# Attention and MoE in one kernel: 512-byte runs for the first loads, w_out behind granules 3 and 4, one exp for two heads, a longer MoE lag

## The chip, the cores and the metric

The kernel runs on one core of a Trainium2 chip. Times are microseconds (us) of device time. Repeated executions of one kernel on one chip mostly agreed within about 1%. A "span" is the length of the one profiled execution; the measured time of that execution is about 1.8 us longer. In the profile, PE is TensorE's matmuls, PEld its weight loads, DVE is VectorE, ACT ScalarE, POOL GpSimd, and SP the engine that issues most transfers of the hardware queue.

## The reference

```python
# attention: B=4, H=8, S=768, D=64; causal window of 96 keys plus 8 global keys, ALiBi bias
scores = q @ k.T / sqrt(D) - slope[h] * dist          # masked outside window and globals
x = softmax(scores) @ v                               # -> (3072 tokens, 512)
# "MoE" with one expert: 512 -> 2048 -> 512
r = relu(x @ w_in)
out = (s * r * r + b) @ w_out
```

Inputs are fp32; the kernel works in bf16 with fp32 sums. The term `b @ w_out` is the same for every token: b times the column sums of w_out, called `bvec` below.

## The kernel before

Tokens are cut into 12 granules of 256; a batch has three. A granule has four "units" (pairs of heads), and a step s treats two units, so a granule takes two steps. q and k of a granule must be transposed before the scores: by TensorE for the first granules, later by DMA. The attention output xn must be transposed to xT for the first MoE product (p1, eight pieces of 8 matmuls per granule). The second product (p2, two halves of 16 matmuls) follows.

```python
    # loads: q/k of granules 0 and 1 as fp32 on two hardware queues, 256-byte runs
    for j in range(2):
        for i in range(GB):
            for n, eng in enumerate((nc.sync, nc.scalar)):
                f = work.tile([P, H, D], F32, name="first", ...)
                eng.dma_start(f[:], rows_of(srcs[n], 0, j * GB + i))
    nc.scalar.preload_act_table_set("natural_log_exp_and_others")
    # ... (constants)
    # everything else by GpSimd's queue, which also casts to bf16, in this order:
    #   v of granules 0, 1;  w_in (4 pieces);  w_out (4 pieces);  granules 2, 3;  later 4, 5, ...

    def post(hi):                      # per head, after the scores of a unit
        nc.scalar.activation(pt[:, 0:ncol], pss[hi][:, 0:ncol], ACT.Exp, scale=QSCALE)
        nc.vector.tensor_tensor(pv, pv, m, ALU.mult)        # mask and bias template

    def step(s, c0, c1, c2):           # c0, c1, c2: MoE pieces put between attention pieces
        j = 2 * s // HP
        last = (2 * s + 2) % HP == 0
        if not last and QK_PE <= j + 2 < NJ:
            qk_by_dma(j + 2)
        run(scores(s + 1))
        ...
        stage_A(2 * s)                 # probabilities @ v, division -> xn
        run(c1)
        stage_A(2 * s + 1)
        run(c2[0:1])
        if last:
            finish_granule(j)          # xT[j]: by TensorE if j < 3, else by DMA; loads granule j+4
        run(c2[1:])

    # ... granules 0, 1 (attention), p1[0], p1[1] with the sums of w_out's rows, p2[0], bvec,
    #     p2[1] mixed with granule 2's attention, granule 3 ...
    for j in range(4, NJ):             # steady part: p1 of the granule just finished
        step(2 * j,     p2[j - 2][0:1], p1[j - 1][0:2], p1[j - 1][2:4])
        step(2 * j + 1, p2[j - 2][1:2], p1[j - 1][4:6], p1[j - 1][6:8])
    run(p2[NJ - 2]); run(p1[NJ - 1]); run(p2[NJ - 1])
```

Each engine executes its instructions in the order in which they are written here.

The softmax here doesn't subtract the row's maximum and nothing guards it: scores larger than these inputs give would overflow.

## Time and profile before

| | before |
|---|---|
| median | 249.51 us (3 runs, 249.46 to 250.19) |
| span | 246.8 us |
| TensorE busy | 218.8 us, 89% |
| VectorE, ScalarE busy | 62%, 43% |

The head of the profile page: span, busy time of the engines, then the busy share of TensorE and its granted clock in tenths, in 40 slices of 6.2 us.

```profile
span 246.8 us, 4975 instructions
...
PE 218.8 (89%) x1955; PEld 145.8 (59%) x1978; DVE 154.1 (62%) x397; ACT 105.6 (43%) x201; POOL 64.5 (26%) x81
...
PE   8768979977987759939989999999999999999993
...
PEclk9995999995899989997999999999999999999999
```

The right half of the TensorE row is nines: there TensorE is the bound, and the timeline repeats one step every 8.0 us. The left half has holes. The waits of TensorE (what it waited for: us in total, times, longest) name the largest:

```profile
PE ps_1297 L387 <- DMA xT<-xn: 4.1, 1, 4.1
PE ps_1557 L387 <- DMA xT<-xn: 4.0, 1, 4.0
PE ps_s L299 <- DVE koff L262: 2.4, 2, 1.9
...
PE ps_1806 L387 <- DMA xT<-xn: 1.1, 1, 1.1
```

A wait has an afterpiece. In TensorE's timeline (start, us, what, count; in brackets the idle time ahead), the 8 matmuls of one p1 piece take 0.87 us from start to start when all is well:

```profile
84.90 0.19 PE L341 MATMUL ps_av<-voff,pt 128*128 128x65 bf16 x1
89.20 1.03 PE L387 MATMUL ps_1297<-xT,w_in_bf 128*128 128x256 bf16 x8 [4.10 <-DMA xT<-xn]
90.07 1.69 PE L387 MATMUL ps_1308<-xT,w_in_bf 128*128 128x256 bf16 x8
91.55 0.26 PE L341 MATMUL ps_av<-vb_88,pt 128*128 128x65 bf16 x1
```

The second piece needs 1.48 us (90.07 to 91.55) because the granted clock fell after the wait.

GpSimd's timeline tells when loads land. It held at most eight loads in flight: before it issues the next, it waits for the one issued eight earlier (the ninth load, at 10.67 us, waits for the first). Here its loads of granule 2 wait for the first and second piece of w_in:

```profile
19.23 0.89 POOL L92 DMA_DIRECT2D nat<-in_k_dram  x1 [1.78 <-DMA w_in_bf<-in_moe_w_in_dram]
22.40 0.88 POOL L92 DMA_DIRECT2D nat<-in_q_dram  x1 [2.28 <-DMA w_in_bf<-in_moe_w_in_dram]
```

**A count of lost time.** To compare kernels by stage I count, in each stretch of 10 us, TensorE's weight loads by kind, multiply each by the time it takes where TensorE is dense (p1 0.109 us, p2 0.2155, scores 0.0345, probabilities times v 0.031, transposes 0.055, all read from dense stretches of the timeline), and call the rest of the 10 us lost. Weight loads are counted because some matmul records are missing from this trace (1955 matmuls against 1978 loads). Before, 45.0 us are lost in the first 140 us: 32.2 ahead of 80 us, 12.8 behind.

### The profile page before, as it was taken

The numbers are of one execution on the slowest core, as the hardware profiler recorded it, in microseconds if no ns is written. First come the engines' busy times: TensorE is split into PE (matmuls) and PEld (weight loads), VectorE is DVE, ScalarE is ACT, GpSimd is POOL, SyncE is SP. The second block draws the span as 40 slices with busy tenths as digits, with TensorE's granted clock in tenths as the row PEclk, the third lists the DMA queues.
The fourth block names the chain that finished last, engine by engine and source line by source line (L and its number), as shares of the span: only waits on it lengthen the run. The fifth ranks groups of instructions, "written<-read, shape, count | busy, mean of one in ns | idle before, by whom it ended". The sixth has DMA issues, their size and how long they took to land.

```text
span 246.8 us, 4975 instructions
## 1 busy us (share of the span) xinstructions
PE 218.8 (89%) x1955; PEld 145.8 (59%) x1978; DVE 154.1 (62%) x397; ACT 105.6 (43%) x201; POOL 64.5 (26%) x81
## 2 busy tenths in 40 slices
PE   8768979977987759939989999999999999999993
PEld 3334968443565445717647756776677666774851
DVE  3478869974799616632566767665577686542431
ACT  0924746006076415603446446634474457330520
POOL 8632428986097500923320000000000000000000
PEclk9995999995899989997999999999999999999999
DMA  8999999999999994999995143252341303113102
GB/s 152 190 186 207 206 197 155 152 177 189 143 138 158 154 160 51 97 153 136 127 107 108 43 78 97 66 108 84 68 106 46 85 3 85 45 43 87 44 0 86
DMA packets 110071, 27.85 MB, mean 113 GB/s; under 512 B 102880, under 2 KB 106976, under 8 KB 110048
## 3 DMA queue, kind: packets, MB, share of 16 engines
q0 software_dynamic: 70784, 12.59, 70.0%
q1 hardware_dynamic: 35104, 13.90, 28.2%
q10 hardware_dynamic: 4160, 1.05, 2.3%
q8 instruction: 15, 0.25, 0.5%
q14 instruction: 8, 0.07, 0.1%
HBM read 27.26 MB, written 6.29 MB: 136 GB/s over the span
## 4 chain that ended last, share of the span: by engine, by line
PE 71%; DMA 13%; DVE 8%; ACT 3%; issue 2%; POOL 1%; SPq 1%; POOLq 0%; ACTq 0%; DVEq 0%
DMA xT<-xn 9%; PE ps_s L299 4%; DMA vb_87<-in_v_dram 4%; PE ps_av L341 4%; ACT pt L310 2%; PE ps_2775 L423 1%; PE ps_1641 L423 1%; PE ps_2290 L423 1%; PE ps_2156 L423 1%; PE ps_1389 L423 1%; PE ps_3027 L423 1%; PE ps_2904 L423 1%; PE ps_2656 L423 1%; PE ps_2531 L423 1%; PE ps_2408 L423 1%
## 5 line engine op out<-in xcount | busy, mean ns | idle before, releaser
L387 PEld LDWEIGHTS <-w_in_bf 128*128 128x128 bf16 x768 | 73.6, 100 | 21.0 <-issue 8.8
L396 DVE TENSOR_TENSOR gT<-gT 128x512 bf16<-128x512 bf16 x96 | 40.4, 424 | 41.8 <-ACT gT L395 39.5
L423 PEld LDWEIGHTS <-gT 128*128 128x128 bf16 x384 | 36.5, 99 | 43.1 <-issue 2.1
L310 ACT ACTIVATE pt<-ps_s 128x512 bf16<-128x512 f32 (+1 forms) x96 | 45.7, 576 | 29.9 <-PE ps_s L299 29.9
L92 POOL DMA_DIRECT2D nat<-in_k_dram x20 | 18.0, 900 | 23.0 <-DMA qk<-nat 15.3
L341 PEld LDWEIGHTS <-pt 128*128 128x128 bf16 x352 | 17.5, 101 | 9.9 <-DVE xn L350 1.9
L92 POOL DMA_DIRECT2D nat<-in_q_dram x20 | 18.0, 898 | 6.1 <-DMA w_in_bf<-in_moe_w_in_dram 3.9
L350 DVE TENSOR_TENSOR xn<-ps_av,rc 128x256 bf16<-128x256 f32 x43 | 18.2, 424 | 1.5
L299 PE MATMUL ps_s<-qk 64*128 64x128 bf16 x224 | 14.9, 228 | 2.8 <-ACT pt L310 2.3
L98 POOL DMA_DIRECT2D vb_88<-in_v_dram x12 | 10.6, 895 | 19.0 <-PE ps_av L341 18.7
L299 PEld LDWEIGHTS <-qk 64*128 64x128 bf16 x224 | 8.2, 97 | 9.5 <-issue 8.3
L98 POOL DMA_DIRECT2D vb_87<-in_v_dram x12 | 11.2, 938 | 6.3 <-DMA w_out_bf<-in_moe_w_out_dram 3.4
L341 PE MATMUL ps_av<-voff,pt 128*128 128x65 bf16 x116 | 11.6, 198 | 0.0
L299 PE MATMUL ps_s<-qk,koff 64*128 64x128 bf16 x128 | 9.4, 237 | 2.4 <-DVE koff L262 2.4
L140 PE MATMUL ps_w<-idle 128*128 128x512 bf16 x30 | 10.0, 478 | 1.5 <-DVE idle L134 1.2
L349 DVE RECIPROCAL rc<-ps_av 128x4 f32<-128x4 f32 x43 | 7.5, 174 | 4.9 <-PE ps_av L341 4.9
L341 PE MATMUL ps_av<-vb_88,pt 128*128 128x65 bf16 x112 | 9.0, 195 | 1.6 <-DVE xn L350 1.6
L404 DVE TENSOR_TENSOR wsum<-wsum,w_out_bf 128x512 f32<-128x512 f32 x14 | 9.6, 685 | 0.2
L341 PE MATMUL ps_av<-vb_87,pt 128*128 128x65 bf16 x88 | 7.8, 198 | 1.2 <-DMA vb_87<-in_v_dram 0.6
L299 PEld LDWEIGHTS <-koff 64*128 64x128 bf16 x128 | 5.5, 104 | 2.8 <-DVE koff L262 2.8
L140 PEld LDWEIGHTS <-idle 128*128 128x128 bf16 x32 | 3.4, 116 | 6.0 <-issue 3.2
L316 DVE TENSOR_TENSOR pt<-pt,tmpl_160 128x512 bf16<-128x512 bf16 (+1 forms) x12 | 4.8, 402 | 3.4 <-ACT pt L310 3.0
(314 smaller groups left out, 363.2 us busy)
## 6 DMA issues: line engine op xcount, KB each, us to landing
out_dram<-o_sb SPq DMA_DIRECT2D x24, 256.0 KB, 2.3
nat<-in_k_dram POOLq DMA_DIRECT2D x20, 128.0 KB, 7.7
nat<-in_q_dram POOLq DMA_DIRECT2D x20, 128.0 KB, 7.5
w_in_bf<-in_moe_w_in_dram POOLq DMA_DIRECT2D x4, 512.0 KB, 15.8
w_out_bf<-in_moe_w_out_dram POOLq DMA_DIRECT2D x4, 512.0 KB, 18.9
vb_87<-in_v_dram POOLq DMA_DIRECT2D x12, 128.0 KB, 10.0
vb_88<-in_v_dram POOLq DMA_DIRECT2D x12, 128.0 KB, 7.2
first<-in_q_dram ACTq DMA_DIRECT2D x4, 256.0 KB, 8.4
```

Source lines behind the costliest of these rows:

```text
L92: nc.gpsimd.dma_start(t[:, n, i, :, :], rows_of(srcs[n], b, g * GB + i))
L98: nc.gpsimd.dma_start(vbuf[b % 2][:, sb, :, 0:D], rows_of(v, b, sb))
L140: nc.tensor.matmul(ps[:], lhsT=idle[:, 0:P], rhs=idle[:], start=True, stop=True)
L299: nc.tensor.matmul(pss[hi][:, oc * P : (oc + 1) * P], lhsT=kt[rows], rhs=qt[rows], start=True, stop=True,)
L310: nc.scalar.activation(pt[:, 0:ncol], pss[hi][:, 0:ncol], ACT.Exp, scale=QSCALE)
L341: nc.tensor.matmul(av[:, i, hi, 0 : D + 1], lhsT=pts[hi][:, c * P : (c + 1) * P], rhs=vv, start=(n == 0), stop=(n == len(terms) - 1),)
L349: nc.vector.reciprocal(rc[:], av[:, :, :, D : D + 1])
L350: nc.vector.tensor_tensor(xn[j][:, :, 2 * hp * D : (2 * hp + 2) * D].rearrange("p i (h d) -> p i h d", d=D), av[:, :, :, 0:D], rc[:].to_br ...
L387: nc.tensor.matmul(ps[:, i, :], lhsT=w_in_bf[:, kc, fc * P : (fc + 1) * P], rhs=xT[j][:, kc, :], start=(kc == 0), stop=(kc == KC - 1),)
L396: nc.vector.tensor_tensor(gs, gs, gs, ALU.mult)
L404: nc.vector.tensor_tensor(wsum[:], a_, w_out_bf[:, i, :], ALU.add)
L423: nc.tensor.matmul(po[:], lhsT=gT[j][:, fc, tb * P : (tb + 1) * P], rhs=w_out_bf[:, fc, :], start=(fc == 0), stop=(fc == FC - 1),)
```

## The change

The intent was to start earlier, to fill TensorE's holes with other work, and to give transposes more time. The parts:

1. Only granule 0's q and k come through the hardware queue (1 MB instead of 2), in 512-byte runs: a partition takes two neighbouring tokens, and the evacuation of the transposes restores the order. ScalarE issues no load, so its table comes first. Granule 1 comes through GpSimd's queue.
2. w_out is loaded behind granules 2 and 3 (numbered 3 and 4 in the title), and the attention of granules 2 and 3 is moved between p1[0] and p1[1]; p2[0] and p2[1] come later.
3. Exp and mask of a unit's two heads are one op each, over two PSUM banks.
4. p1 and p2 lag half a granule to a granule further behind attention; granule 3's xT is made by TensorE as well. For granules 0 to 2 every second square goes to ScalarE, as do some evacuations.

```diff
-    N_HW = 2
...
-                f = work.tile([P, H, D], F32, name="first", tag="first", bufs=2 * GB * N_HW)
-                eng.dma_start(f[:], rows_of(srcs[n], 0, j * GB + i))
+    for h2 in range(2):
+        for n in range(2):
+            f = work.tile([P, H // 2, GB * D], F32, name="first", tag="first", bufs=4)
+            nc.sync.dma_start(f[:], pairs_of(srcs[n], 0, h2 * H // 2, H // 2))
...
-    for j in range(N_HW):
-        nat_tile(j)
-        load_v(j)
+    nat_tile(0)
+    load_v(0)
+    load_granule(1)
     for i in range(4):
         load_w_in(i, 4)
+    load_granule(2)
+    load_granule(3)
     for i in range(4):
         load_w_out(i, 4)
-    load_granule(2)
-    load_granule(3)
...
-            nc.scalar.activation(pt[:, 0:ncol], pss[hi][:, 0:ncol], ACT.Exp, scale=QSCALE)
+            nc.scalar.activation(pt[:, :, 0:ncol], ps[:, :, 0:ncol], ACT.Exp, scale=QSCALE)
...
-        nc.vector.tensor_copy(t[:], ps[:])
+        nc.scalar.copy(t[:], ps[:])
...
-        nc.vector.tensor_tensor(gs, gs, gs, ALU.mult)
+        if sq_on_act:
+            nc.scalar.activation(gs, gs, ACT.Square)
+        else:
+            nc.vector.tensor_tensor(gs, gs, gs, ALU.mult)
...
-    X_PE = 3
+    X_PE = 4
...   (the written order of the first 75 us; its end:)
+    load_granule(4)
+    load_granule(5)
+    run(scores(6))
+    qk_by_dma(4)
+    step(6, p1[2][0:1], sums[0:2] + p1[2][1:3], p1[2][3:4] + sums[2:6])
+    qk_by_dma(5)
+    step(7, p1[2][4:5], sums[6:8] + p1[2][5:7], p1[2][7:8] + sums[8:13])
+    (p2[0], the last sums, bvec)
...
-    for j in range(4, NJ):
-        step(2 * j, p2[j - 2][0:1], p1[j - 1][0:2], p1[j - 1][2:4])
-        step(2 * j + 1, p2[j - 2][1:2], p1[j - 1][4:6], p1[j - 1][6:8])
+    step(8, p2[1][0:1], p1[3][0:2], p1[3][2:4])
+    step(9, p2[1][1:2], p1[3][4:6], p1[3][6:8])
+    step(10, p2[2][0:1], p2[2][1:2], [])
+    step(11, p2[3][0:1], p1[4][0:2], p1[4][2:4])
+    for j in range(6, NJ):
+        step(2 * j, p2[j - 3][1:2], p1[j - 2][4:6], p1[j - 2][6:8])
+        step(2 * j + 1, p2[j - 2][0:1], p1[j - 1][0:2], p1[j - 1][2:4])
```

`sums` are 15 additions that build the column sums of w_out on VectorE. Note step 7: it opens with the scores of granule 4, the first granule whose q and k are transposed by DMA.

More of the change, by code (lines that the diff above doesn't have):

```diff
@@ L58 @@
     work = ctx.enter_context(tc.tile_pool(name="work", bufs=3))
-    ppool = ctx.enter_context(tc.tile_pool(name="ppool", bufs=8))
+    ppool = ctx.enter_context(tc.tile_pool(name="ppool", bufs=4))
     gpool = ctx.enter_context(tc.tile_pool(name="gpool", bufs=4))
     xpool = ctx.enter_context(tc.tile_pool(name="xpool", bufs=3))
-    ps_sc = ctx.enter_context(tc.tile_pool(name="ps_sc", bufs=4, space=bass.MemoryType.PSUM))
+    ps_sc = ctx.enter_context(tc.tile_pool(name="ps_sc", bufs=2, space=bass.MemoryType.PSUM))
     ps_av = ctx.enter_context(tc.tile_pool(name="ps_av", bufs=1, space=bass.MemoryType.PSUM))
@@ L66 @@
     ctx.enter_context(tc.manual_schedule())
+    nc.scalar.preload_act_table_set("natural_log_exp_and_others")
+    QK_PE = 4
+    X_PE = 4
     NB = S // P
@@ L85, in rows_of, with pairs_of @@
         return src[b, :, sb * P : (sb + 1) * P, :].rearrange("h p d -> p h d")
+    def pairs_of(src, j, h0=0, nh=H):
+        b, g = divmod(j, NGR)
+        return src[b, h0 : h0 + nh, g * GT : (g + 1) * GT, :].rearrange(
+            "h (p s) d -> p h (s d)", s=GB
+        )
     def load_granule(j):
@@ L98, in load_v @@
             nc.gpsimd.dma_start(vbuf[b % 2][:, sb, :, 0:D], rows_of(v, b, sb))
-    N_HW = 2
     first_f32 = {}
-    for j in range(N_HW):
-        for i in range(GB):
-            for n, eng in enumerate((nc.sync, nc.scalar)):
-                f = work.tile([P, H, D], F32, name="first", tag="first", bufs=2 * GB * N_HW)
-                eng.dma_start(f[:], rows_of(srcs[n], 0, j * GB + i))
-                first_f32[j, n, i] = f
-    nc.scalar.preload_act_table_set("natural_log_exp_and_others")
+    for h2 in range(2):
+        for n in range(2):
+            f = work.tile([P, H // 2, GB * D], F32, name="first", tag="first", bufs=4)
+            nc.sync.dma_start(f[:], pairs_of(srcs[n], 0, h2 * H // 2, H // 2))
+            first_f32[h2, n] = f
     w_in_bf = const.tile([P, KC, DF], BF16, name="w_in_bf")
@@ L173 @@
     )
-    for j in range(N_HW):
-        nat_tile(j)
-        load_v(j)
+    nat_tile(0)
+    load_v(0)
+    load_granule(1)
     for i in range(4):
         load_w_in(i, 4)
+    load_granule(2)
+    load_granule(3)
     for i in range(4):
         load_w_out(i, 4)
-    load_granule(2)
-    load_granule(3)
     nc.vector.tensor_copy(base[:, 0, :], rel[:, 0:P])
@@ L187, with template_rest, cast_first @@
     nc.vector.memset(base[0:NG, 2, :], -float(NL))
-    tmpl = []
+    tmpl = const.tile([P, H, 5, P], BF16, name="tmpl")
     for h in range(H):
-        t = const.tile([P, 3, P], BF16, name=f"tmpl{h}", tag=f"tmpl{h}")
         slope = float(2.0 ** (-8.0 * (h + 1) / H))
-        nc.scalar.activation(t[:], base[:], ACT.Exp, scale=slope)
-        tmpl.append(t)
-    def cast_first(j):
-        for i in range(GB):
-            for n in range(2):
-                nc.vector.tensor_copy(nat[j][:, n, i, :, :], first_f32[j, n, i][:])
+        nc.scalar.activation(tmpl[:, h, 0:3, :], base[:], ACT.Exp, scale=slope)
+    def template_rest():
+        nc.vector.tensor_copy(tmpl[:, :, 3, :], tmpl[:, :, 2, :])
+        nc.vector.tensor_copy(tmpl[:, :, 4, :], tmpl[:, :, 1, :])
+    def cast_first(h2):
+        hs = slice(h2 * H // 2, (h2 + 1) * H // 2)
+        for n in range(2):
+            nc.vector.tensor_copy(
+                nat[0][:, n, :, hs, :],
+                first_f32[h2, n][:].rearrange("p h (s d) -> p s h d", s=GB),
+            )
     for vb in vbuf:
@@ L223, in qk_tile, with qk_by_pe @@
         return qk[b]
-    def qk_by_pe(j, h2s=range(HP // 2)):
+    def qk_by_pe(j, h2s=range(HP // 2), evac=(nc.vector.tensor_copy, nc.vector.tensor_copy)):
         b, g = divmod(j, NGR)
@@ L238, in qk_by_pe @@
                         )
-            nc.vector.tensor_copy(
-                t[:, :, g * GB : (g + 1) * GB, 2 * h2 : 2 * h2 + 2, :], ps[:]
-            )
+            for n in range(2):
+                dst = t[:, n, g * GB : (g + 1) * GB, 2 * h2 : 2 * h2 + 2, :]
+                if j == 0:
+                    evac[n](
+                        dst.rearrange("p b c (m s) -> p c b m s", s=GB),
+                        ps[:, n].rearrange("p s c (b m) -> p c b m s", b=GB),
+                    )
+                else:
+                    evac[n](dst, ps[:, n])
     def qk_by_dma(j):
@@ L286, in stage_S @@
         ncol = 3 * P if first else 4 * P
-        pss = [ps_sc.tile([P, 4 * P], F32, name="ps_s", tag="sc") for _ in range(2)]
-        pts = [ppool.tile([P, 4 * P], BF16, name="pt", tag="pt") for _ in range(2)]
-        st[u] = pts
+        ps = ps_sc.tile([P, 2, 4 * P], F32, name="ps_s", tag="sc")
+        pt = ppool.tile([P, 2, 4 * P], BF16, name="pt", tag="pt")
+        st[u] = pt
         r0 = g * GB
-        plan = [(t[:, 0, r0 + i, hp, :], t[:, 1, r0 + i, hp, :]) for i in range(GB)]
+        plan = [(i, t[:, 0, r0 + i, hp, :], t[:, 1, r0 + i, hp, :]) for i in range(GB)]
         if first:
-            plan.append((t[:, 0, 0, hp, :], t[:, 1, 1, hp, :]))
+            plan.append((2, t[:, 0, 0, hp, :], t[:, 1, 1, hp, :]))
         else:
-            plan += [(koff[j][:, i, hp, :], t[:, 1, r0 + i, hp, :]) for i in range(GB)]
-        for oc, (kt, qt) in enumerate(plan):
+            plan = [
+                (0,) + plan[0][1:],
+                (3,) + plan[1][1:],
+                (1, koff[j][:, 0, hp, :], t[:, 1, r0, hp, :]),
+                (2, koff[j][:, 1, hp, :], t[:, 1, r0 + 1, hp, :]),
+            ]
+        for oc, kt, qt in plan:
             for hi in range(2):
@@ L299, in stage_S @@
                 nc.tensor.matmul(
-                    pss[hi][:, oc * P : (oc + 1) * P],
+                    ps[:, hi, oc * P : (oc + 1) * P],
                     lhsT=kt[rows],
@@ L305, in stage_S, with post @@
                 )
-        def post(hi):
-            h = 2 * hp + hi
-            pt = pts[hi]
-            nc.scalar.activation(pt[:, 0:ncol], pss[hi][:, 0:ncol], ACT.Exp, scale=QSCALE)
-            if first:
-                pv, m = pt[:, 0:ncol].rearrange("p (a c) -> p a c", c=P), tmpl[h][:]
-            else:
-                pv = pt[:].rearrange("p (a i c) -> p a i c", i=GB, c=P)
-                m = tmpl[h][:, 1:3, :].unsqueeze(2).to_broadcast((P, 2, GB, P))
-            nc.vector.tensor_tensor(pv, pv, m, ALU.mult)
-        return [lambda: post(0), lambda: post(1)]
+        def post():
+            nc.scalar.activation(pt[:, :, 0:ncol], ps[:, :, 0:ncol], ACT.Exp, scale=QSCALE)
+            c0 = 0 if first else 1
+            m = tmpl[:, 2 * hp : 2 * hp + 2, c0 : c0 + ncol // P, :]
+            pv = pt[:, :, 0:ncol]
+            nc.vector.tensor_tensor(pv, pv, m.rearrange("p h a c -> p h (a c)"), ALU.mult)
+        return [post]
     def stage_A(u, pool=None):
@@ L323, in stage_A @@
         first = g == 0
-        pts = st.pop(u)
+        pt = st.pop(u)
         vn = vbuf[b % 2]
@@ L331, in stage_A @@
             xn[j] = xpool.tile([P, GB, DM], BF16, name="xn", tag="xn")
+        dcol, ocol = ((0, 1), (None, 2)) if first else ((0, 3), (1, 2))
         for i in range(GB):
@@ L334, in stage_A @@
                 h = 2 * hp + hi
-                terms = [(i, vn[:, g * GB + i, h, 0 : D + 1])]
+                terms = [(dcol[i], vn[:, g * GB + i, h, 0 : D + 1])]
                 if not first:
-                    terms.append((GB + i, voff[j][:, i, h, 0 : D + 1]))
+                    terms.append((ocol[i], voff[j][:, i, h, 0 : D + 1]))
                 elif i == 1:
-                    terms.append((GB, vn[:, 0, h, 0 : D + 1]))
+                    terms.append((2, vn[:, 0, h, 0 : D + 1]))
                 for n, (c, vv) in enumerate(terms):
@@ L342, in stage_A @@
                         av[:, i, hi, 0 : D + 1],
-                        lhsT=pts[hi][:, c * P : (c + 1) * P],
+                        lhsT=pt[:, hi, c * P : (c + 1) * P],
                         rhs=vv,
@@ L376, in x_by_dma, with moe_p1 @@
             nc.sync.dma_start_transpose(t[:, :, i * P : (i + 1) * P], xn[j][:, i, :])
-    def moe_p1(j, fp):
+    def moe_p1(j, fp, sq_on_act=False):
         if j not in gT:
@@ L395, in moe_p1 @@
         nc.scalar.activation(gs, ps[:], ACT.Relu)
-        nc.vector.tensor_tensor(gs, gs, gs, ALU.mult)
+        if sq_on_act:
+            nc.scalar.activation(gs, gs, ACT.Square)
+        else:
+            nc.vector.tensor_tensor(gs, gs, gs, ALU.mult)
     bvec = const.tile([P, DM], F32, name="bvec")
@@ L447, in moe_p2 @@
         p2_out(j, tb)
-    p1 = {j: [lambda j=j, f=f: moe_p1(j, f) for f in range(FC // 2)] for j in range(NJ)}
+    p1 = {
+        j: [lambda j=j, f=f: moe_p1(j, f, j < 3 and f % 2 == 1) for f in range(FC // 2)]
+        for j in range(NJ)
+    }
     p2 = {j: [lambda j=j, t=t: moe_p2(j, t) for t in range(GB)] for j in range(NJ)}
@@ L464, in scores @@
         return posts
-    QK_PE = 4
-    X_PE = 3
     def finish_granule(j):
@@ L473, in finish_granule @@
             x_by_dma(j)
-        if j + 4 < NJ:
-            load_granule(j + 4)
+        if 6 <= j + 3 < NJ:
+            load_granule(j + 3)
     def step(s, c0, c1, c2):
@@ L480, in step @@
         last = (2 * s + 2) % HP == 0
-        if not last and QK_PE <= j + 2 < NJ:
+        if not last and j >= 4 and j + 2 < NJ:
             qk_by_dma(j + 2)
         run(scores(s + 1))
-        if last and j + 1 < NJ:
-            make_voff(j + 1)
+        if not last:
+            make_voff(j)
         run(c0)
@@ L495, in step @@
         run(c2[1:])
-    warm(20)
+    both = (nc.vector.tensor_copy, nc.scalar.copy)
+    warm(14)
     cast_first(0)
-    qk_by_pe(0)
-    run(scores(0))
+    qk_by_pe(0, [0])
+    cast_first(1)
+    qk_by_pe(0, [1])
+    posts = scores(0)
+    run(posts)
     warm(4)
@@ L506 @@
     run(posts)
-    cast_first(1)
-    warm(4)
+    qk_by_pe(1, evac=both)
+    template_rest()
+    make_koff(1)
     stage_A(2)
     stage_A(3, ps_h)
-    qk_by_pe(1)
-    make_koff(1)
+    posts = scores(2)
     x_by_pe(0)
-    run(scores(2))
+    run(posts)
     make_voff(1)
-    warm(4)
+    run(p1[0][0:2])
     posts = scores(3)
     stage_A(4)
-    stage_A(5, ps_h)
+    stage_A(5)
     run(posts)
-    run(p1[0][0:2])
+    run(p1[0][2:4])
     stage_A(6)
-    run(p1[0][2:4])
+    run(p1[0][4:6])
     stage_A(7)
-    run(p1[0][4:6])
+    run(p1[0][6:7])
     x_by_pe(1)
-    tail = p1[1][0:6] + p1[0][6:8] + p1[1][6:8]
-    for i, c in enumerate(tail):
-        c()
-        sums[i]()
+    run(p1[0][7:8])
+    run(p1[1][0:2])
+    qk_by_pe(2, evac=both)
+    make_koff(2)
+    run(p1[1][2:3])
+    run(scores(4))
+    make_voff(2)
+    run(p1[1][3:4])
+    posts = scores(5)
+    stage_A(8)
+    run(p1[1][4:5])
+    stage_A(9)
+    run(posts)
+    run(p1[1][5:6])
+    qk_by_pe(3, evac=both)
+    stage_A(10)
+    run(p1[1][6:7])
+    stage_A(11)
+    run(p1[1][7:8])
+    x_by_pe(2)
+    load_granule(4)
+    load_granule(5)
+    run(scores(6))
+    qk_by_dma(4)
     nq = FC // 4
+    step(6, p1[2][0:1], sums[0:2] + p1[2][1:3], p1[2][3:4] + sums[2:6])
+    qk_by_dma(5)
+    step(7, p1[2][4:5], sums[6:8] + p1[2][5:7], p1[2][7:8] + sums[8:13])
     for qt in range(4):
@@ L534 @@
             p2_mm(0, tb, qt * nq, (qt + 1) * nq)
-    run(sums[len(tail) :])
+    run(sums[13:])
     emit_bvec()
@@ L538 @@
         p2_out(0, tb)
-    load_granule(4)
-    load_granule(5)
-    p2_mm(1, 0, 0, FC // 2)
-    qk_by_pe(2, [0])
-    p2_mm(1, 0, FC // 2, FC)
-    p2_out(1, 0)
-    qk_by_pe(2, [1])
-    make_koff(2)
-    run(scores(4))
-    make_voff(2)
-    qk_by_dma(4)
-    posts = scores(5)
-    p2_mm(1, 1, 0, FC // 2)
-    stage_A(8)
-    stage_A(9, ps_h)
-    run(posts)
-    p2_mm(1, 1, FC // 2, FC)
-    p2_out(1, 1)
-    stage_A(10)
-    stage_A(11, ps_h)
-    qk_by_pe(3)
-    finish_granule(2)
-    run(scores(6))
-    step(6, p1[2][0:1], p1[2][1:3], p1[2][3:4])
-    step(7, p1[2][4:5], p1[2][5:7], p1[2][7:8])
-    for j in range(4, NJ):
-        step(2 * j, p2[j - 2][0:1], p1[j - 1][0:2], p1[j - 1][2:4])
-        step(2 * j + 1, p2[j - 2][1:2], p1[j - 1][4:6], p1[j - 1][6:8])
+    step(8, p2[1][0:1], p1[3][0:2], p1[3][2:4])
[5 more added lines that the diff above has]
+        step(2 * j + 1, p2[j - 2][0:1], p1[j - 1][0:2], p1[j - 1][2:4])
+    run(p2[NJ - 3][1:2])
+    run(p1[NJ - 2][4:8])
     run(p2[NJ - 2])
```

## The prediction

> **What bounds the kernel now.** From about 116 us on, TensorE. Windows of five microseconds show it busy 4.95 to 5.00 us at clock 1.00; the timeline repeats one step (scores, one half of the second MoE product, four pieces of the first) every 8.0 us; 24 steps are 192 us, and the transposes on TensorE add about 5. The rest of the 246.8 us span is lost early. The first MoE matmul starts at 25.4 us. The waits of TensorE show 4.1 and 4.0 us for the DMA transposes of xT at 85 to 89 and 107 to 111 us (1.1 and 0.4 later), each followed by 1 to 1.5 us at a lower clock; there are 1.9 us for koff at 54 to 56, and smaller ones.
>
> Until about 62 us the loads are never idle. GpSimd's waits show when they land: w_in's four pieces at 19.1, 22.3, 24.6, 27.2, w_out's at 29.8 to 37.8 us (2.6 us each), then each 128 KB q, k or v load about 0.9 to 1.0 us after the one before.
>
> **The change.**
> 1. Start: 1 MB instead of 2 MB through the hardware queues, in 512-byte runs, and ScalarE issues none (its table load came at 6.3 us, the first exp at 10.9). The Trainium skill, "DMA: Bandwidth & Descriptors", Specifications, names 512 B as the least size for line rate; this trace shows only the 256 B loads, about 160 GB/s for the first megabyte. I expect first exp near 8.5 us and the first MoE matmul near 17 us.
> 2. Exp of two heads: one op. "ScalarE: Activation LUTs", What ACT_TABLE_LOAD costs, gives 186 ns + 0.833 ns per column, 613 ns for 512; the trace's 128x512 Relu takes 0.60. Estimate 1.04 us instead of 1.2 per pair, some 7 us of ScalarE. At 43% busy, that is worth nothing.
> 3. Longer lag, and granule 3 transposed on TensorE: xT has over 8 us from issue to use, so about 9.6 us of waits and 3 us of low clock vanish.
> 4. w_out after granules 3: attention of granules 2 and 3 runs between the first products of granules 0 and 1. But granule 4's loads now stand behind the same bytes, and TensorE reaches its scores without having done the second products of granules 0 and 1 (14 us).
>
> **Sum.** w_in's first piece at about 15 us (estimate), seven more pieces at 2.6, sixteen small loads at 1.0: k and q of granule 4 land near 49, their DMA transposes (1.2 us issue each, 4.7 to landing) near 55. TensorE has 30 us of work before scores of granule 4 and gets there near 48: a new stall of about 7 us. koff of granule 4 also blocks VectorE in that time; its backlog of w_out sums and divisions costs TensorE some 3 us more, and low clock 1 to 2. From those scores on, the trace of before gives 154 us of pure TensorE work, plus 14 for the moved products: 55.5 + 168 + 5 + 4 (last output) = 232 us span, 234 to 235 measured. That stall absorbs nearly everything ahead of it.
>
> I predict 234 us, 8 in 10 between 227 and 242; faster by over 2% 0.93, within 2% 0.06, slower 0.01.
>
> **What would show it.** First MoE matmul at 17 us; no waits on xT over 1 us; a TensorE wait of 4 to 10 us before the scores of granule 4, ended by koff or the DMA of qk; a step of 8.0 us after 100 us.
>
> **What would make it wrong.** Loads faster than estimated: no stall, 226. Transposes of qk slowed by loads, or a late load of granule 6 or 7: 240 or more.

## The result, and the profile after

| | before | after |
|---|---|---|
| median | 249.85 us (4 runs, 249.46 to 250.38) | 236.38 us (4 runs, 235.75 to 237.07) |
| ratio | | 0.946, 95% interval 0.9422 to 0.9499 |
| span | 246.8 us | 234.1 us |
| first piece of p1 starts | 25.4 us | 20.8 us |
| first exp starts | 10.94 us | 10.87 us |
| ScalarE busy | 105.6 us | 116.2 us |
| lost ahead of 80 us / from 80 to 140 us | 32.2 / 12.8 us | 32.8 / 0.2 us |

A ratio is the mean time of one kernel's fast runs over that of the other's fast runs of the same rounds, so it is not quite the ratio of the medians.

The head of the page after the change:

```profile
span 234.1 us, 4849 instructions
...
PE 213.4 (91%) x1972; PEld 143.6 (61%) x1972; DVE 141.8 (61%) x334; ACT 116.2 (50%) x175; POOL 68.2 (29%) x85
...
PE   7477897859789899999999999999999999999993
...
PEclk9975899997999999999999999999999999999999
```

TensorE is dense from 80 us on instead of 116. The last row of the table holds the main finding: the whole gain lies behind 80 us. The rebuilt first 80 us lose as much as the old ones. By tens of us, the lost time is:

```
from (us)    0   10   20   30   40   50   60   70 | 80   90  100  110  120
before     8.7  7.5  3.7  1.4  0.1  4.6  4.2  2.0 | 4.2  1.7  3.1  2.4  1.4
after      9.0  6.5  3.7  1.9  3.8  4.2  2.3  1.4 | 0.0 -0.1  0.0  0.2  0.0
```

TensorE's waits after the change; no wait on xT by DMA is among them:

```profile
PE ps_av L362 <- DVE xn L371: 2.8, 3, 1.6
PE ps_s L323 <- ACT pt L332: 2.6, 3, 1.8
...
PE ps_s L323 <- DMA qk<-nat: 0.5, 1, 0.5
```

The predicted stall at the scores of granule 4 shows as a wait of 0.5 us, not 7. TensorE's timeline ahead of it:

```profile
51.88 0.34 PE L323 MATMUL ps_s<-qk 64*128 64x128 bf16 x6 [0.36 <-ACT pt L332]
52.16 1.79 PE L408 MATMUL ps_846<-xT,w_in_bf 128*128 128x256 bf16 x8
53.74 0.54 PE L362 MATMUL ps_av<-vb_89,pt 128*128 128x65 bf16 x6
54.09 1.82 PE L408 MATMUL ps_873<-xT,w_in_bf 128*128 128x256 bf16 x8
55.75 1.04 PE L408 MATMUL ps_884<-xT,w_in_bf 128*128 128x256 bf16 x8
...
58.50 0.23 PE L323 MATMUL ps_s<-qk 64*128 64x128 bf16 x2 [0.50 <-DMA qk<-nat]
```

Two p1 pieces start 1.58 and 1.66 us before what follows them, nearly twice the usual 0.87. The windows of five microseconds (length, busy time of PE, PEld, DVE, ACT, POOL with counts, then the granted clock, DMA share, GB/s) show the low clock there and at the first p1 pieces:

```profile
20.00:25.00 5.00, 4.21 (x30) 2.88 (x31) 2.80 (x6) 3.78 (x5) 1.83 (x2) 0.50 1.57 189
50.00:55.00 5.00, 3.46 (x31) 2.52 (x31) 2.62 (x6) 3.83 (x6) 0.69 (x1) 0.73 2.57 147
```

The Trainium skill, "TensorE: Matmul & The Clock Gate", What's actually happening, describes two clock states, full and half, chosen by how busy the array has lately been; the 0.50 and the nearly doubled times agree.

### The profile page after: what moved, and what is told of

Its sections match the earlier page's. It is cut to its first block, busy times and chain, and to the rows that moved or that the text cites. A ratio compares the mean times of both kernels' runs of the same rounds, so it can differ in the third digit from the quotient of the medians.

```text
span 234.1 us, 4849 instructions
## 1 busy us (share of the span) xinstructions
PE 213.4 (91%) x1972; PEld 143.6 (61%) x1972; DVE 141.8 (61%) x334; ACT 116.2 (50%) x175; POOL 68.2 (29%) x85
## 3 DMA queue, kind: packets, MB, share of 16 engines
q1 hardware_dynamic: 31968, 13.64, 29.8%
## 4 chain that ended last, share of the span: by engine, by line
PE 80%; DVE 10%; ACT 7%; issue 1%; DVEq 0%
PE ps_s L323 4%; PE ps_av L362 4%; PE ps_w L147 3%; ACT pt L332 2%; ACT gT L416 2%; DVE wsum L428 2%; DVE pt L336 2%; PE ps_1575 L447 2%; PE ps_1452 L447 2%; PE ps_2758 L447 2%; PE ps_2638 L447 2%; PE ps_2522 L447 2%; PE ps_2406 L447 2%; PE ps_2294 L447 2%; PE ps_2171 L447 2%; PE ps_2062 L447 2%
## 5 line engine op out<-in xcount | busy, mean ns | idle before, releaser
L420 DVE TENSOR_TENSOR gT<-gT 128x512 bf16<-128x512 bf16 x84 | 35.7, 425 | 32.6 <-ACT gT L416 30.7
L332 ACT ACTIVATE pt<-ps_s 128x1024 bf16<-128x1024 f32 (+1 forms) x48 | 42.9, 953 | 17.0 <-PE ps_s L323 17.0
L336 DVE TENSOR_TENSOR pt<-pt,tmpl 128x1024 bf16<-128x1024 bf16 (+1 forms) x48 | 30.7, 647 | 16.8 <-ACT pt L332 15.6
L102 POOL DMA_DIRECT2D nat<-in_k_dram x22 | 20.3, 922 | 14.9 <-DMA qk<-nat 9.7
L102 POOL DMA_DIRECT2D nat<-in_q_dram x22 | 20.1, 914 | 3.1 <-DMA w_in_bf<-in_moe_w_in_dram 1.6
L371 DVE TENSOR_TENSOR xn<-ps_av,rc 128x256 bf16<-128x256 f32 x46 | 19.5, 425 | 1.6
L323 PE MATMUL ps_s<-qk 64*128 64x128 bf16 x224 | 13.6, 227 | 5.0 <-ACT pt L332 2.6
L108 POOL DMA_DIRECT2D vb_89<-in_v_dram x12 | 10.6, 895 | 19.5 <-PE ps_av L362 17.3
L418 ACT ACTIVATE gT<-gT 128x512 bf16<-128x512 bf16 x12 | 7.6, 630 | 0.4
L147 PE MATMUL ps_w<-idle 128*128 128x512 bf16 x18 | 6.4, 520 | 1.2 <-DVE idle L141 1.2
L246 PE MATMUL ps_t<-ident_bf,nat 128*128 128x128 bf16 x64 | 5.0, 232 | 2.0 <-DVE nat L208 2.0
```

Source lines behind the costliest of these rows:

```text
L102: nc.gpsimd.dma_start(t[:, n, i, :, :], rows_of(srcs[n], b, g * GB + i))
L108: nc.gpsimd.dma_start(vbuf[b % 2][:, sb, :, 0:D], rows_of(v, b, sb))
L147: nc.tensor.matmul(ps[:], lhsT=idle[:, 0:P], rhs=idle[:], start=True, stop=True)
L323: nc.tensor.matmul(ps[:, hi, oc * P : (oc + 1) * P], lhsT=kt[rows], rhs=qt[rows], start=True, stop=True,)
L332: nc.scalar.activation(pt[:, :, 0:ncol], ps[:, :, 0:ncol], ACT.Exp, scale=QSCALE)
L336: nc.vector.tensor_tensor(pv, pv, m.rearrange("p h a c -> p h (a c)"), ALU.mult)
```

## The experiments

All twelve runs were correct. Three batches ran on three chips; the median of the kernel before was 249.24, 249.05 and 250.42 us on them. The changed kernel itself ran again in the third batch. Its ratio is 0.946 in its first measurement and 0.9432 in the second, so differences below about 0.5% between batches are not read.

| run | median us | ratio to before | 95% interval | lost before / after 80 us |
|---|---|---|---|---|
| b_lag | 238.94 | 0.9577 | 0.9521 to 0.9634 | 32.3 / 3.4 |
| a_nolag | 243.54 | 0.9738 | 0.9667 to 0.9809 | 33.1 / 7.4 |
| a_256 | 237.09 | 0.9512 | 0.9462 to 0.9562 | 33.8 / 0.9 |
| a_split | 236.59 | 0.9487 | 0.9434 to 0.954 | 33.8 / 0.6 |
| a_sq | 237.66 | 0.9535 | 0.9503 to 0.9567 | 33.9 / -0.2 |
| a_g4 | 237.36 | 0.9532 | 0.9496 to 0.9568 | 34.4 / 1.9 |
| a_g4_sq | 238.46 | 0.9543 | 0.9493 to 0.9594 | (slow) |
| a_pool | 240.49 | 0.9645 | 0.9603 to 0.9687 | 35.0 / 0.6 |
| a_again | 235.88 | 0.9432 | 0.9388 to 0.9476 | 32.1 / 0.1 |
| a_warm | 237.43 | 0.9486 | 0.9442 to 0.9531 | 34.2 / 0.7 |
| a_pesum | 234.89 | 0.9371 | 0.9316 to 0.9427 | 28.1 / -0.3 |
| a_pesum_warm | 235.26 | 0.942 | 0.9363 to 0.9477 | 29.8 / 0.2 |

The medians include three slow runs (one each of a_nolag, a_g4_sq and a_pesum); the ratios leave them out. In the last column empty matmuls count as lost time, and the 3.0 us of column sums that two runs add on TensorE count as work.

### b_lag: the lag alone, in the kernel before

```diff
-    X_PE = 3
+    X_PE = 4
...
-    for j in range(4, NJ):
-        step(2 * j, p2[j - 2][0:1], p1[j - 1][0:2], p1[j - 1][2:4])
-        step(2 * j + 1, p2[j - 2][1:2], p1[j - 1][4:6], p1[j - 1][6:8])
+    step(8, p2[2][0:1], p1[3][0:2], p1[3][2:4])
+    step(9, [], p1[3][4:6], p1[3][6:8])
+    step(10, p2[2][1:2], [], [])
+    step(11, p2[3][0:1], p1[4][0:2], p1[4][2:4])
+    (then the changed kernel's loop from granule 6, and its end)
```

> The kernel before with the longer MoE lag and X_PE = 4 alone; loads, exp and first 75 us as before. My theory (the lag removes 9.6 us of waits on xT and about 3 us of low clock after them, and nothing else is in the way): about 11 us less than before, 238 to 240 us, no TensorE wait on xT above 0.5 us, TensorE dense from about 80 us. Rival A (the loads that slowed those DMA transposes also hold the next granules' q and k, so the wait only moves to the scores or koff): within 4 us of before, with new waits before the scores of granules 4 to 6. Rival B (most of the change's gain comes from the reordered first 60 us): at most 5 us gained.

Measured: 238.94 us, 10.3 us below the median of before. The first 80 us are those of before. Its waits:

```profile
PE ps_av L341 <- DVE xn L350: 5.0, 3, 2.0
PE ps_s L299 <- DVE koff L262: 2.4, 2, 1.9
```

No wait on xT by DMA is left. Two of the three waits on xn (2.00 and 1.15 us, ending at 94 and 102 us) are new: with p2[0] and p2[1] already done, my steps 9 and 10 have too little TensorE work to cover the exp and the division. Rival A and rival B both fall. A few lines of the change carry 10.3 of the 13.5 us, and the rest of it is worth about 3 us on top. b_lag takes the longer lag and granule 3's transposes on TensorE together; it does not tell how much each is worth.

### a_nolag: the changed kernel with the old lag

```diff
-    step(10, p2[2][0:1], p2[2][1:2], [])
-    step(11, p2[3][0:1], p1[4][0:2], p1[4][2:4])
-    (the loop from granule 6)
+    for j in range(5, NJ):
+        step(2 * j, p2[j - 3][0:1], p1[j - 1][0:2], p1[j - 1][2:4])
+        step(2 * j + 1, p2[j - 3][1:2], p1[j - 1][4:6], p1[j - 1][6:8])
```

> The changed kernel with the old lag from granule 5 on (first product of granule j-1 in the steps of granule j). My theory: waits on xT come back at granules 4 and 5 (step 10 and 12), 2 to 4 us each, and low clock after them: 241 to 246 us. Rival (in the changed kernel the loads end earlier, near 105 us instead of 120, so the transposes are fast and the old lag would do): within 1.5 us of 236.4.

Measured: ratio 0.9738 against 0.946, so about 7 us lost (three fast runs; the fourth was slow). TensorE's timeline:

```profile
111.35 0.34 PE L362 MATMUL ps_av<-vb,pt 128*128 128x65 bf16 x6
117.01 3.57 PE L408 MATMUL ps<-xT,w_in_bf 128*128 128x256 bf16 x16 [5.32 <-DMA xT<-xn]
120.37 0.54 PE L362 MATMUL ps_av<-vb,pt 128*128 128x65 bf16 x6
```

One wait of 5.3 us came back, and the two p1 pieces behind it take 3.36 us instead of 1.75. 5.3 and 1.6 are 6.9 us, and the count finds 7.0 us lost between 110 and 120 us. I had expected waits at two granules; there was one, longer. The lag is needed in the changed kernel too. (X_PE stays 4 here, so granule 3's wait does not return.)

### a_256: the same first megabyte in 256-byte runs

```diff
-            f = work.tile([P, H // 2, GB * D], F32, name="first", tag="first", bufs=4)
-            nc.sync.dma_start(f[:], pairs_of(srcs[n], 0, h2 * H // 2, H // 2))
+            f = work.tile([P, GB, H // 2, D], F32, name="first", tag="first", bufs=4)
+            for i in range(GB):
+                nc.sync.dma_start(f[:, i], rows_of(srcs[n], 0, i)[:, h2 * H // 2 : (h2 + 1) * H // 2, :])
 (cast and evacuation in natural token order, as for the other granules)
```

> The changed kernel with its first megabyte in 256-byte runs (eight DMAs by head half and block on the same queue, natural token order, dense evacuation of the transposes). Theory 1 (a later start is absorbed, since the scores of granule 4 wait for the DMA transposes of its q and k anyway): within 0.7 us of 236.4, first MoE matmul up to 2 us later than 20.8 us. Theory 2 (TensorE arrives at those scores only 0.7 us before the data, so every delay of the start beyond that shows in the end): 1 to 3 us slower. If the strided evacuation of the 512-byte form (1.29 us for two against 0.87) costs more than the runs save, it is 0.5 us faster.

Measured: 0.9512 against 0.946 and 0.9432, intervals overlapping; 0.5 to 0.8% slower at best guess. VectorE's last cast of the first granule starts at 11.35 us, with 2.13 us of wait for its load; in the changed kernel the last two start at 7.70 us without one. The shorter runs do land later: the last transfer at 11.3 us instead of 7.0 (7.1 to 8.1 in the other runs with long ones). They are also eight transfers instead of four, so the length of the runs is not tested alone. Of this delay, some 1 to 2 us reach the end, if the difference is real; that leaves both theories open. The first p1 piece starts at 23.3 us, but that number is loose: kernels with the changed kernel's start untouched have it between 20.1 and 22.6 us, with granted clocks of 0.50 to 1.00 between 10 and 15 us.

### a_split: exp and mask per head

```diff
-            nc.scalar.activation(pt[:, :, 0:ncol], ps[:, :, 0:ncol], ACT.Exp, scale=QSCALE)
+            for hi in range(2):
+                nc.scalar.activation(pt[:, hi, 0:ncol], ps[:, hi, 0:ncol], ACT.Exp, scale=QSCALE)
+                (and the mask of this head)
```

> The changed kernel with exp and mask per head (two ops of 512 columns instead of one of 1024; same PSUM tile). My prediction (joint exp is worth nothing, ScalarE is not the bound): within 0.7 us of 236.4, ScalarE busy up by about 6 us over the whole run. Rival (ScalarE is the busiest engine from 25 to 50 us of the changed kernel, 4.5 to 4.8 of each 5 us, and sets TensorE's pace there): 1.5 to 3 us slower, scores of granule 4 later than 58.5 us by that much.

Measured: 0.9487, within 0.3% of the first measurement of the changed kernel and 0.6% above the second. ScalarE is busy 119.3 us instead of 116.2, half of the rise that I expected. The joint op is worth nothing that can be measured here, as predicted. The rival of a ScalarE-bound stretch from 25 to 50 us gets no support.

### a_sq, a_g4, a_g4_sq: what holds the scores of granule 4

These ask whether ScalarE (squares) or the DMA of granule 4's q and k sets the pace ahead of the scores of granule 4.

```diff
 a_sq and a_g4_sq:
-        j: [lambda j=j, f=f: moe_p1(j, f, j < 3 and f % 2 == 1) ...
+        j: [lambda j=j, f=f: moe_p1(j, f, False) ...
 a_g4 and a_g4_sq:
     load_granule(3)
-    for i in range(4):
-        load_w_out(i, 4)
...
     x_by_pe(0)
+    load_granule(4)
+    for i in range(4):
+        load_w_out(i, 4)
...
     x_by_pe(2)
-    load_granule(4)
     load_granule(5)
```

> The changed kernel with all squares back on VectorE (none on ScalarE for granules 0 to 2). Theory D (the DMA transposes of granule 4's q and k set when its scores start, 58.5 us): TensorE comes to these scores 2 to 4 us earlier and waits there for the DMA instead, total within 0.7 us of 236.4. Theory S (ScalarE sets the pace up to there and the DMA would have been in time): 2 to 4 us faster. If VectorE becomes the bound instead: slower.

> The changed kernel with granule 4's loads ahead of w_out instead of behind. Theory D: TensorE is only 0.5 us early at the scores of granule 4, so 0.5 us faster, with no wait on the DMA of qk left; low clock and ScalarE unchanged. Rival (loads do not matter there at all): the same within noise.

> Both: squares on VectorE and granule 4's loads ahead of w_out. Theory D: the two limits stand one behind the other, so together they give more than the sum of each alone: 2 to 4 us faster than 236.4, scores of granule 4 at 54 to 56 us. Rival (ScalarE is not what delays TensorE there; the low clock and the dependency chain are): within 1 us of the run with the loads alone. w_out lands later here (near 52 us): a wait of VectorE's sums for it would eat part.

Measured: 0.9535, 0.9532 and 0.9543, so all three are slower than the changed kernel by 0.7 to 1.2% (against 0.946 and 0.9432; the changed kernel did not run on this chip, so a part may be the chip's). That was not expected, and its cause is open. In a_sq TensorE comes to these scores at the same time as before and then waits longer for the DMA:

```profile
57.92 0.23 PE L323 MATMUL ps_s<-qk 64*128 64x128 bf16 x2
59.66 0.23 PE L323 MATMUL ps_s<-qk 64*128 64x128 bf16 x2 [1.51 <-DMA qk<-nat]
```

The unchanged kernel waits as long there in its second profile (a_again, 1.7 us). Theory S, that ScalarE sets the pace, gets no support, but Theory D's earlier TensorE did not come either; and the squares went to VectorE, which may have cost what ScalarE saved. In a_g4 the queue's four transposes of granule 4 are issued from 38.38 us on, and the wait on them is gone; but TensorE reaches the scores only at 59.37 us:

```profile
59.37 0.28 PE L321 MATMUL ps_s<-qk 64*128 64x128 bf16 x4
59.49 0.28 PE L321 MATMUL ps_s<-qk,koff 64*128 64x128 bf16 x4
```

It lost about 0.9 and 0.3 us in two p1 pieces to a low clock at 43.8 and 46.0 us (0.83 on average from 40 to 50 us) that the changed kernel does not have there, and later it waits 2.8 us for VectorE instead of 1.6. So with the wait on the DMA gone nothing is gained: TensorE itself is no earlier. Two cautions. This profile is of the slowest of a_g4's six runs (239.19 us), and its first p1 piece starts at 22.6 us instead of 20.8. And the limit did not move far: with w_out's loads now beside them, the four transposes took 8.3 to 13.3 us from issue to landing, and the last landed at 56.5 us, only 2.0 us earlier than in the changed kernel. My expectation that the two changes together would gain more than their sum failed, since moving the squares did not make TensorE earlier.

### a_pool: the sums of w_out on GpSimd

```diff
-        nc.vector.tensor_tensor(wsum[:], a_, w_out_bf[:, i, :], ALU.add)
+        nc.gpsimd.tensor_tensor(wsum[:], a_, w_out_bf[:, i, :], ALU.add)
 (all 15 right after load_granule(5))
```

> The changed kernel with the 15 sums of w_out's rows on GpSimd (ahead of granule 6's loads) instead of VectorE. My prediction's step (VectorE's backlog of sums costs TensorE some 3 us after the scores of granule 4): 2 to 3.5 us faster, TensorE's waits on VectorE at 63 and 65 us gone. Rival (the sums only fill VectorE's idle time, and other things hold TensorE there): no change. GpSimd's sums may take over 1.5 us each and hold its loads of granule 6, or collide with VectorE[...]: then slower, with a wait for the loads of granule 6 or for the bias vector.

Measured: 0.9645, some 2% slower than the changed kernel. The sums take 1.22 us each on GpSimd (0.69 on VectorE), and VectorE suffers at the same time. Its masks of granule 3's scores in a_pool:

```profile
50.81 5.68 DVE L336 TENSOR_TENSOR pt<-pt,tmpl 128x768 bf16<-128x768 bf16 x4 [2.55 <-ACT pt L332]
56.41 1.37 DVE L420 TENSOR_TENSOR gT<-gT 128x512 bf16<-128x512 bf16 x1
```

and the same instructions in the changed kernel:

```profile
51.16 2.66 DVE L336 TENSOR_TENSOR pt<-pt,tmpl 128x768 bf16<-128x768 bf16 x4 [2.54 <-ACT pt L332]
54.61 0.43 DVE L420 TENSOR_TENSOR gT<-gT 128x512 bf16<-128x512 bf16 x1 [0.79 <-ACT gT L416]
```

The Trainium skill, "SBUF — State Buffer", Who interferes with whom, says that a VectorE instruction with two SBUF inputs contends with a GpSimd instruction that reads SBUF, and that the order of issue decides which of the two is blocked. The trace agrees that they contend: while GpSimd's sums ran, from 52.0 to 72.1 us, a square of 0.43 us took 1.37 us, longer by most of one GpSimd sum, and the four masks took 5.68 us instead of 2.66. So this run cannot tell what VectorE's backlog costs; it replaced one load by another.

### a_again, a_warm, a_pesum, a_pesum_warm: low clock and backlog, side by side

```diff
 a_warm and a_pesum_warm (empty matmuls into a scratch bank):
     qk_by_pe(0, [0])
+    warm(6)
     cast_first(1)
     qk_by_pe(0, [1])
+    warm(4)
...
     stage_A(3, ps_h)
+    warm(5)
     posts = scores(2)
     x_by_pe(0)
+    warm(4)
 a_warm only:
     run(scores(6))
+    warm(7)
 a_pesum and a_pesum_warm (no sums on VectorE; ones @ w_out on TensorE instead):
     run(scores(6))
+    for fc in range(FC):
+        nc.tensor.matmul(ps[:], lhsT=ones_bf[:], rhs=w_out_bf[:, fc, :], start=(fc == 0), stop=(fc == FC - 1))
+    nc.vector.tensor_scalar_mul(bvec[:], ps[:], b_bc[:])
```

> The changed kernel itself once more, on the same chip and in the same rounds as the three below: 235.7 to 237.1 us if chips do not matter.

> The changed kernel with 26 more matmuls on an empty tile, put where TensorE waits at 6.5, 9.2, 17, 19.7 and 50 us, so that it is not sparse before the first products of granules 0 and 2. Theory (the first four product blocks run at 1.65 to 1.9 us instead of 0.87 because TensorE was sparse just before; 1.75 us at 21 to 24 us and 1.9 us at 52 to 56): granted clock above 0.9 from 20 to 25 and from 50 to 55 us, 1.5 to 3 us faster, and if only the first comes, its gain is eaten by the wait on the DMA of qk at the scores of granule 4, which then grows to 1.5 to 2 us. Rival (the low clock is not due to these gaps): clocks as before, and 0 to 2 us slower for the matmuls added.

> The changed kernel with the column sums of w_out made on TensorE (16 matmuls with a matrix of ones right after the scores of the second half of granule 3's first step, where TensorE waits 2.1 us and then runs at low clock) instead of 15 additions on VectorE. 3.45 us of TensorE work added, 0.43 taken away. Theory (VectorE's backlog of sums costs TensorE 3 to 4 us between 59 and 79 us; the added work fills a wait of 2.1 us and keeps the clock up, 1.9 us): waits on VectorE at 63, 65 and 78 us gone, loss from 50 to 80 us down from 7.5 to about 4, 232 to 234 us. Rival (the sums only fill VectorE's idle time): 1 to 3 us slower, as TensorE is the bound.

> Both: sums on TensorE, and the added empty matmuls up to 20 us (not the late ones). If the theories of both hold and the wait on the DMA of qk does not eat the early gain: 231 to 233 us, the fastest of all; if that wait does: as the run with the sums alone within 0.7 us, with 1.5 us or more of wait on the DMA of qk. If the empty matmuls do nothing: as the run with the sums alone.

**a_again** measured 0.9432 and a mean of 236.0 us, as the first time. Its profile has a wait of 1.7 us on the DMA of qk where the first profile has 0.5. Its waits on VectorE at 63, 65 and 78 us are 0.51, 0.65 and 0.37 us where the first profile has 1.65, 0.65 and 0.96.

**a_warm** is the run that settles the stall. The clock did as expected:

```profile
20.00:25.00 5.00, 3.62 (x54) 2.88 (x52) 3.49 (x10) 4.97 (x7) 1.75 (x2) 1.00 1.47 195
50.00:55.00 5.00, 4.31 (x50) 3.64 (x50) 3.84 (x10) 4.32 (x8) 1.17 (x2) 1.00 2.32 153
55.00:60.00 5.00, 0.23 (x2) 0.19 (x2) 4.20 (x8) 0.71 (x2) 0.00 (x0) 0.89 1.96 127
60.00:65.00 5.00, 4.73 (x37) 3.55 (x37) 2.67 (x6) 2.54 (x3) 4.17 (x5) 0.50 1.63 133
```

It is 1.00 in both early stretches, and TensorE comes to the scores of granule 4 at 54.5 us instead of 57.8. Then it stands still from 55 to 60 us:

```profile
53.41 1.04 PE L408 MATMUL ps<-xT,w_in_bf 128*128 128x256 bf16 x8
55.91 0.23 PE L323 MATMUL ps_s<-qk 64*128 64x128 bf16 x2 [1.45 <-DMA qk<-nat]
60.27 0.29 PE L323 MATMUL ps_s<-qk 64*128 64x128 bf16 x2 [4.13 <-DMA qk<-nat]
60.33 0.45 PE L323 MATMUL ps_s<-qk,koff 64*128 64x128 bf16 x4
```

It waits 5.6 us for the DMA, and the clock of the next five microseconds is 0.50. The kernel is not faster for the 3.3 us gained, but 1.4 us slower (237.4 against 236.0 us in the mean, same chip and rounds). The wall of the prediction is real, at 58.5 to 60.3 us. The changed kernel does not bump into it hard only because its TensorE is slow on the way.

**a_pesum** is the fastest: fast runs of 234.5 us in the mean against 236.0 of a_again, five and six runs, standard deviations 1.0 and 0.8, so about 1.5 us, though the two intervals against before overlap. It is below the expected gain of 2 to 4 us. Lost time between 50 and 80 us is 2.7 us against 7.2 in a_again, with 3.0 us of TensorE work added. Where a_again waits and then runs at low clock,

```profile
50.94 0.34 PE L323 MATMUL ps_s<-qk 64*128 64x128 bf16 x6 [1.78 <-ACT pt L332]
...
53.20 3.34 PE L408 MATMUL ps<-xT,w_in_bf 128*128 128x256 bf16 x16
...
59.47 0.23 PE L323 MATMUL ps_s<-qk 64*128 64x128 bf16 x2 [1.71 <-DMA qk<-nat]
...
63.46 0.36 PE L362 MATMUL ps_av<-vb,pt 128*128 128x65 bf16 x6 [0.51 <-DVE xn L371]
```

a_pesum has

```profile
50.71 3.63 PE L433 MATMUL ps_b<-w_out_bf,ones_bf 128*128 128x512 bf16 x16
54.27 0.51 PE L323 MATMUL ps_s<-qk 64*128 64x128 bf16 x12
54.71 1.05 PE L408 MATMUL ps<-xT,w_in_bf 128*128 128x256 bf16 x8
...
63.82 0.36 PE L362 MATMUL ps_av<-vb,pt 128*128 128x65 bf16 x6 [0.51 <-DVE xn L371]
```

The wait on VectorE near 63 us is 0.51 us in both, with the sums on VectorE and without. Of the 4.5 us between 7.2 and 2.7, 3.6 lie ahead of 60 us, where a wait is filled and the clock stays up. How much of the rest is the backlog of sums, this run does not tell.

**a_pesum_warm** gave 235.7 us in the mean (six runs, standard deviation 1.6), not faster than a_pesum; it waits 2.4 us for the DMA of qk. The wait fits the second of its expected outcomes; the mean is 1.2 us above that of a_pesum, where at most 0.7 was expected.

Left open: the early warm matmuls together with granule 4's loads ahead of w_out, which would move both limits at once, was not run (a_g4's landing at 56.5 us, against a_warm's arrival at 54.5, suggests that a wait would remain); a_pesum needs w_out by 50 us and so cannot simply be joined with it.

## Why the prediction was right, and where not

The measured 236.38 us lies within 227 to 242, 2.4 us above the forecast. Point by point:

1. **The lag (step 3): right.** About 9.6 us of waits and 3 us of low clock were to vanish. The count shows 12.8 us lost behind 80 us before and 0.2 after; b_lag, which changes nothing else, gained 10.3 us while adding 3.2 us of waits of its own.
2. **The joint exp (step 2): right that it is worth nothing.** a_split is within 0.3%. The estimate from "ScalarE: Activation LUTs" agrees with the trace: 1.04 us for 1024 columns against a median of 1.018 measured, 0.61 for 512 against 0.60. But ScalarE's busy time rose by 10.6 us instead of falling by 7, since I had left the moved squares and evacuations out of that sum. a_split shows 3 us for the joint op itself.
3. **The start (step 1): mis-sized.** "First exp near 8.5 us and the first MoE matmul near 17 us" became 10.87 and 20.8. The template work no longer stands before the first exp, but the chain through casts, transposes and evacuations on one VectorE does; and the first p1 pieces then run at a clock of 0.50. Neither was in my sum. In the count, the first 30 us lose 19.2 us instead of 19.9.
4. **The stall (step 4): its place was right, its size wrong, and that the sum held is in part luck.** "TensorE ... gets there near 48: a new stall of about 7 us." k and q of granule 4 land at 46.7 to 49.2 us, about as predicted, but their transposes take 6.9 to 7.7 us from issue to landing instead of 4.7, so the last lands at 58.5 us (predicted 55). TensorE arrives at 57.8. Of its 9.8 us of delay, 3.8 are the later start and about 3.3 the low clock at 21 to 24 and 52 to 56 us (four p1 pieces of 1.58 to 1.84 us instead of 0.87); the rest is short waits on ScalarE and VectorE. Almost the whole wait was spent beforehand. a_warm, with the clock at 1.00, has TensorE there at 54.5 us (1.0 of the 3.3 us is an earlier first piece, at 19.8) and shows the predicted wait: 5.6 us. The later of the two arrivals counts, and it was predicted 3 us too early; that TensorE, 9.8 us late, came no later than the data is luck.
5. **koff holding up VectorE: wrong.** koff of granule 4 ran at 55.5 us without a wait of its own.
6. **The backlog of sums: not shown.** The predicted 3 us compare with waits of TensorE on VectorE of 1.65, 0.65 and 0.96 us at 63, 65 and 78 us in the first profile, but of 0.51, 0.65 and 0.37 us in that of a_again, the same kernel. a_pesum, without the sums, still has 0.51 and 0.50 us. By these single profiles the sums cost between 0.5 and 2.3 us.
7. **The sum.** 55.5 + 168 + 5 + 4 was predicted. Measured: scores at 58.5, last matmul's end near 230.3, span 234.1, so 171.8 for the middle part against 173, and 3.8 for the end. The scores came 3.0 us later and the middle and the end took 1.4 us less, which gives the 1.6 us between 232.5 and 234.1.

Where the intended gain of the first part went: the earlier start and the reordering won back 2.5 us between 60 and 80 us and lost 3.7 between 40 and 50. b_lag and the changed kernel differ by about 3 us, and 3.2 us of that are b_lag's own thin steps. Nothing in these runs shows a net gain of the new first 80 us.

## What to carry to other kernels

When work is moved earlier, look for the next thing that arrives at a fixed time (here, transposes by DMA behind a queue of loads, at 58 to 60 us): up to it, a saving can turn into a wait, as in a_warm. Count the lost time by stage before and after, since the same total hides where it came from: here a few lines in the steady part gave most of the gain, and a long rewrite of the start none that could be shown. Fill a known wait with needed work rather than with empty matmuls; the sums as matmuls in a hole gained 1.5 us where moving them to GpSimd lost 2%.

## What the Trainium skill lacked or had wrong

- "TensorE: Matmul & The Clock Gate", HAM oscillation, gives the rule against idle gaps over about 3.4 us. In the changed kernel the clock was 0.50 from 20 to 25 us although no wait of TensorE between 15 and 21 us exceeded 1.1 us; it was busy 2.99 of the 5 us before. Filling those short gaps brought the clock to 1.00 (a_warm). The page's next section speaks of short idle times in a kernel that cycles PSUM banks, but not of what share of busy time is enough.
- No page that I read has the time of a DMA transpose beside loads: before the change, the two transposes of xT issued at 80.7 and 82.0 us, among loads, took 6.8 and 7.1 us from issue to landing, against a median of 2.5 us over the run; in a_g4, those of q and k beside the loads of w_out took up to 13.3 us.
- "DMA: Bandwidth & Descriptors", Specifications, names 512 B as the size for line rate. The runs agree in direction (the last cast of the first megabyte begins at 7.7 us with 512-byte runs, 11.35 with 256-byte ones, which were also twice as many transfers), but how little of such a gain reaches the end is a matter of the kernel: 1 to 2 us at most here.
